# A new hand-written order for the five instruction queues of a clustered attention kernel with a spatial gating layer

## The chip, the cores and the metric

The kernel runs on one core of one Trainium2 chip. The metric is the device time of one execution in microseconds (us). The kernel before took 648.02 us, the median of 3 runs (647.39 to 654.46). TensorE is called PE here, VectorE DVE, ScalarE ACT, GpSimd POOL, and SyncE, which issues nearly all DMAs, SP.

## The reference

Two stages follow each other. First an attention in which a query sees only the keys of its own cluster (4 batches, 8 heads, 768 rows, 64 columns), then a gated layer on the joined heads.

```python
q_assign = argmax(einsum('bhsd,hcd->bhsc', q_n, c_n))   # 16 clusters a head
k_assign = argmax(einsum('bhsd,hcd->bhsc', k_n, c_n))
mask = q_assign[:, :, :, None] == k_assign[:, :, None, :]
scores = where(mask, 0.125 * q @ k.T, -1e9)
attn = softmax(scores)
x = (attn @ v)            # heads joined: 4 x 768 x 512
h = relu(x @ w_in)        # 512 -> 1024
u, v = h[..., :512], h[..., 512:]
v_n = (v - mean(v)) / sqrt(var(v) + 1e-6)
v_s = einsum('ts,bsd->btd', w_spatial, v_n) + b_spatial
out = (u * v_s) @ w_out
```

## The kernel before, in words

The work is cut into 16 head pairs, four a batch, numbered 0 to 15. For each pair `prep` loads q, k and v, splits them into float16 high and low parts, finds the clusters by small matmuls (lines 708 to 710, "logits") and DVE steps (lines 727 to 731), and has ACT write the one-hot codes into `ohx` (lines 739 and 740). For the first heads `shifts` computes a bound on the scores first: matmuls of line 826, one DVE maximum each (line 833), a last reduction (line 845) and its way into `hq` (lines 846, 849, 863, 864). `attend` then makes the attention in tiles of 128 rows by 768 columns, six a head. There are two kinds of tile:

- 108 tiles of the earlier heads: scores (lines 923 and 925), exponential on ACT (929), float16 copy on ACT (931), low part on POOL (932), then 18 matmuls with v (937, "values").
- 84 tiles of the later heads (the list `ROW`), which take their maximum over a row of the scores: scores (lines 887 and 889), DVE maximum (892 to 894), exponential on ACT into a `p32` buffer (895), copy on ACT (897), low part on POOL (898), a transposing DMA issued by SP from `pt` back into the same `p32` buffer (903), then 18 matmuls with v (907). In the trace `p32` is called p. There are four `p32` buffers: the exponential of a tile has to wait until the values of the tile four before it have been read.

`mlp` does the gated layer of a batch once its four pairs have their transposed x. Its matmuls all have line 982 (a helper), in chunks of six matmuls of 128x512: v and u (from xT and win), the spatial product (from vn and wsp, then DVE 1046, ACT 1047, POOL 1048 and a transposing DMA 1049), and the output product (from gT, in the last batch from a `pt` buffer, and wou; then ACT 1059 and the output DMA 1060). The chunks of batch b are spread between the attention tiles of batch b+1; those of the last batch stand alone at the end.

Every piece of work is recorded as an operation with its engine (`op`), and nothing is issued until `plan.run()`. A table `ORDER` then gives, for each of the five queues, the order in which its operations are issued, as numbers: the k-th recorded operation of that engine. PE has 799 operations, ACT 738, DVE 908, POOL 294, SP 355. `run` walks through the queues with its own estimate of start times, which only decides which PSUM buffer (of four `acc` and two `sc`) an operation gets; the order within a queue is the table's.

```python
own = [o for o in self.ops if o.eng == e]
queue[e] = [own[int(k)] for k in ORDER.get(e, "").split()][::-1]
```

An engine runs its queue in order. An operation that waits holds up all that stands behind it on its engine.

Of the kernel before, what the change touches and what calls it, by code (L numbers as in the profile page):

```python
# [151 lines left out]
""",  # L152
    "ACT": """
# [16 lines left out]
""",  # L170
    "DVE": """
# [960 lines left out]
```

## Time and profile before

| what | value |
|---|---|
| time, median of 3 runs | 648.02 us (647.39 to 654.46) |
| time of the profiled execution | 652.16 us |
| its span, first to last instruction | 650.4 us |
| PE busy | 598.9 us, 92% of the span |
| ACT, DVE, POOL busy | 456.1 us, 436.4 us, 429.7 us |
| mean granted clock of PE, as a share of 2.4 GHz | 0.99 |

The profile is one execution on the chip. The table says how long each engine worked, not what set the end: PE is the busiest, and the 51 us in which it did nothing are spread over the span. The rows further down show where.

### The profile page before, as it was taken

Reading aid. Unit: us, or ns where it says so; the run is one execution under the profiler, and the core shown is the slowest. Engines: PE = TensorE matmul, PEld = TensorE weight load, DVE = VectorE, ACT = ScalarE, POOL = GpSimd, SP = SyncE. Lnnn points to the kernel's source line nnn. Section 1 sums busy time; section 2 is a strip of 40 time slices with the busy share of each in tenths; the row PEclk is TensorE's granted clock in tenths of the full one; section 3 lists DMA queues with packets and bytes.
Section 4 is the critical chain, followed back from the end, with each engine's and each line's share of the span. In section 5 each row is a group of like instructions: output and inputs, shape, how many; then the busy total and the mean of one; then the engine's idle time right before and its main releaser. Section 6 shows DMA issues by size and latency. Waiting matters only on the chain.

```text
span 650.4 us, 16379 instructions
## 1 busy us (share of the span) xinstructions
PE 598.9 (92%) x6509; PEld 355.9 (55%) x6509; DVE 436.4 (67%) x935; ACT 456.1 (70%) x713; POOL 429.7 (66%) x305
## 2 busy tenths in 40 slices
PE   3798998799999999988999999889989999899996
PEld 2475766566555655555665566555555555444442
DVE  7899999998879884768785646658556556123110
ACT  5688999798777767768789788776868787233122
POOL 2468999789477956668688879665868677323210
PEclk9999999799989999999999999999999999899999
DMA  6566676656744999899868799999999999900215
GB/s 196 126 171 158 164 160 141 163 129 156 175 84 142 189 209 175 180 170 196 164 147 164 142 228 180 203 188 163 186 200 195 197 187 179 153 33 16 43 41 145
DMA packets 225645, 101.38 MB, mean 156 GB/s; under 512 B 210320, under 2 KB 211936, under 8 KB 225568
## 3 DMA queue, kind: packets, MB, share of 16 engines
q1 hardware_dynamic: 221824, 93.65, 72.9%
q10 hardware_dynamic: 3744, 6.69, 3.1%
q8 instruction: 51, 0.84, 0.5%
q14 instruction: 26, 0.21, 0.1%
HBM read 27.63 MB, written 6.29 MB: 52 GB/s over the span
## 4 chain that ended last, share of the span: by engine, by line
PE 35%; DMA 14%; ACT 4%; issue 3%; DVE 3%; POOL 2%; SPq 1%; POOLq 0%; ACTq 0%; DVEq 0%
PE acc L982 22%; DMA p<-pt 11%; PE acc L907 5%; PE sc L887 2%; PE sc L889 2%; PE acc L937 2%; DMA gT<-ghl 2%; ACT p L895 1%; DMA pt<-ghl 1%; POOL pt L898 1%; DVE rs L892 1%; ACT pt L897 1%; PE sc L923 1%; PE sc L925 1%; PE acc L826 0%
## 5 line engine op out<-in xcount | busy, mean ns | idle before, releaser
L932 POOL TENSOR_TENSOR pt<-p,pt 128x768 f16<-128x768 f32 x108 | 185.5, 1736 | 38.7 <-ACT pt L931 20.3
L898 POOL TENSOR_TENSOR pt<-p,pt 128x768 f16<-128x768 f32 x84 | 139.6, 1665 | 67.7 <-ACT pt L897 41.2
L982 PE MATMUL acc<-win,xT 128*128 128x512 f16 x576 | 134.4, 379 | 0.3 <-DMA xT<-xhl 0.3
L892 DVE TENSOR_REDUCE rs<-sc 128x1 f32<-128x768 f32 x84 | 80.1, 954 | 55.3 <-PE sc L889 53.3
L895 ACT ACTIVATE p<-sc,rs 128x768 f32<-128x768 f32 x84 | 83.0, 990 | 43.7 <-DVE rs L894 22.6
L833 DVE TENSOR_REDUCE nm<-acc 128x1 f32<-128x512 f32 (+1 forms) x162 | 104.8, 680 | 12.1 <-PE acc L826 11.8
L982 PE MATMUL acc<-vn,wsp 128*128 128x512 f16 x432 | 101.1, 379 | 0.0
L929 ACT ACTIVATE p<-sc 128x768 f32<-128x768 f32 x108 | 85.6, 805 | 14.2 <-PE sc L925 7.0
L931 ACT CAST pt<-p 128x768 f16<-128x768 f32 x108 | 87.7, 828 | 2.4 <-PE acc L937 2.0
L982 PEld LDWEIGHTS <-xT 128*128 128x128 f16 x576 | 54.9, 97 | 60.9 <-DMA xT<-xhl 0.8
L937 PEld LDWEIGHTS <-pt 128*128 128x128 f16 x1944 | 71.2, 99 | 10.8 <-issue 1.2
L937 PE MATMUL acc<-vhl,pt 128*128 128x65 f16 (+1 forms) x1944 | 75.4, 195 | 0.0
L907 PEld LDWEIGHTS <-p 128*128 128x128 f16 x1512 | 55.2, 97 | 33.8 <-DMA p<-pt 21.5
L907 PE MATMUL acc<-vhl,p 128*128 128x65 f16 x1512 | 59.4, 193 | 13.4 <-DMA p<-pt 13.3
L897 ACT CAST pt<-p 128x768 f16<-128x768 f32 x84 | 69.7, 830 | 1.7 <-PE acc L937 0.3
L826 PE MATMUL acc<-hq 80*128 80x512 f16 (+1 forms) x216 | 60.4, 351 | 10.8 <-DVE nm L833 4.4
L982 PEld LDWEIGHTS <-wsp 128*128 128x128 f16 x432 | 40.9, 97 | 44.8
L982 PE MATMUL acc<-wou,gT 128*128 128x512 f16 x216 | 53.1, 388 | 3.8 <-DMA gT<-ghl 3.8
L923 PE MATMUL sc<-hq,lo 128*128 128x512 f16 x216 | 55.6, 340 | 0.5 <-ACT p L929 0.4
L925 PE MATMUL sc<-hq 81*128 81x512 f16 x216 | 55.3, 338 | 0.2 <-DVE hq L864 0.2
L1048 POOL TENSOR_TENSOR ghl<-u,ghl 128x512 f16<-128x512 f32 x24 | 28.3, 1186 | 40.7 <-ACT ghl L1047 39.4
L1046 DVE SCALAR_TENSOR_TENSOR u<-acc,bsp,u 128x512 f32<-128x512 f32 x24 | 18.0, 748 | 51.5 <-PE acc L982 51.3
(125 smaller groups left out, 873.8 us busy)
## 6 DMA issues: line engine op xcount, KB each, us to landing
raw<-in_kqT_dram SPq DMA_DIRECT2D x15, 768.0 KB
vraw<-in_vp_dram SPq DMA_DIRECT2D x16, 384.0 KB
hq<-hq SPq DMA_DIRECT2D x15, 384.0 KB
out_dram<-gT ACTq DMA_DIRECT2D x18, 256.0 KB
hq<-lo SPq DMA_DIRECT2D x16, 192.0 KB
lo<-hq SPq DMA_DIRECT2D x16, 192.0 KB
wraw<-in_wsT_dram SPq DMA_DIRECT2D x6, 384.0 KB
vn<-in_w_in_dram SPq DMA_DIRECT2D x4, 512.0 KB
```

Of the source, the lines that this page charges most:

```text
L833: V.tensor_reduce(out=nm.t[:, t, k:k + 1] if n == 1 else nm.t[:, t:t + n, k], in_=src, axis=AX.X, op=ALU.max, negate=True)
L892: o = op("DVE", 0.95, lambda sc=sc, rs=rs: V.tensor_reduce(out=rs.t[:, 0:1], in_=sc.t[:, 0:S], axis=AX.X, op=ALU.max, negate=True), after= ...
L895: o = op("ACT", 0.99, lambda sc=sc, p32=p32, rs=rs: A.activation(out=p32.t, in_=sc.t[:, 0:S], func=AF.Exp, bias=rs.t[:, 2:3], scale=rs.t[: ...
L897: o = op("ACT", 0.83, lambda pt=pt, p32=p32: A.copy(out=pt.t[:, 0, :], in_=p32.t), after=[o], use=[p32], new=[pt], key=K_HI)
L898: o = op("POOL", 1.65, lambda pt=pt, p32=p32: G_.tensor_tensor(out=pt.t[:, 1, :], in0=p32.t, in1=pt.t[:, 0, :], op=ALU.subtract), after=[o ...
L907: T.matmul(out=av.t[:, k * (D + 1):k * (D + 1) + w], lhsT=rt()[:, c, :], rhs=rhs, skip_group_check=True, **f)
L923: T.matmul(out=sc.t[:, cs], lhsT=lo.t[:, h, ks], rhs=hq.t[:, 2, h, cs], start=True, stop=False)
L929: o = op("ACT", 0.81, lambda sc=sc, p32=p32: A.activation(out=p32.t, in_=sc.t[:, 0:S], func=AF.Exp, bias=P_LOG * LN2, scale=SC_UNIT), afte ...
L931: o = op("ACT", 0.83, lambda pt=pt, p32=p32: A.copy(out=pt.t[:, 0, :], in_=p32.t), after=[o], use=[p32], new=[pt], key=K_HI)
L932: o = op("POOL", 1.65, lambda pt=pt, p32=p32: G_.tensor_tensor(out=pt.t[:, 1, :], in0=p32.t, in1=pt.t[:, 0, :], op=ALU.subtract), after=[o ...
L937: T.matmul(out=av.t[:, t * (D + 1):t * (D + 1) + w], lhsT=lhsT, rhs=rhs, skip_group_check=True, **f)
L982: T.matmul(out=acc.t, lhsT=lr[m][0], rhs=lr[m][1], start=(m == 0), stop=(m == n - 1))
```

## The change

All five lists of numbers in `ORDER` are replaced by others. The order was searched for anew over replays in which DMA landings, loads and issue times were scattered. No operation, tile, buffer or constant is changed: each list holds the same numbers as before. The last two lines of POOL's list stand for the rest (the lists are 3094 numbers in all):

```diff
     "POOL": """
...
-270 257 272 273 264 274 275 276 277 219 220 271 221 278 279 281 280 222 282 283 284 285 287 286 288 289 290 292 291 293
+270 272 257 273 264 274 275 276 277 271 219 220 221 278 222 279 280 281 282 283 284 285 287 286 288 289 290 291 292 293
```

What this moves is seen in the queues themselves. Three places follow.

First place: ACT near the start, where pair 1's codes (lines 740 and 739, which read `acc1` and so give it back) meet the load of pair 2 (line 668 reads `raw`, which a DMA fills). The kernel before:

```order
L846 ACTIVATE shx0_84<-nl_361 128x6
L849 ACTIVATE shx0_84<-nl_361 128x6 x2
L668 ACTIVATE hq_380<-raw_310 128x768
L740 ACTIVATE ohx_83<-acc1_111 128x6x2x16
L739 ACTIVATE ohx_83<-acc1_111 128x6x2x16
L929 ACTIVATE p32_390<-sc1_109 128x768
```

The changed kernel at the same place:

```order
L793 ACTIVATE wl0_93<-w32_259 2x2x65
L740 ACTIVATE ohx_83<-acc1_111 128x6x2x16
L739 ACTIVATE ohx_83<-acc1_111 128x6x2x16
L668 ACTIVATE hq_383<-raw_312 128x768
L929 ACTIVATE p32_400<-sc0_108 128x768
```

The two code writes moved from behind line 668 to before it.

Second place: PE in pair 14, the first tile of its first head, just ahead of that tile's values (line 907; p32_8239 and p32_8241 are the tile's buffer in the one kernel and the other). The kernel before:

```order
L889 LDWEIGHTS hq_6512
L889 MATMUL sc1_109<-hq_6512 128x512
L889 LDWEIGHTS hq_6512
L889 MATMUL sc1_109<-hq_6512 128x256
L907 LDWEIGHTS p32_8239
L907 MATMUL acc0_110<-vhl0_87,p32_8239 128x65
```

The changed kernel, directly ahead of the same tile's values:

```order
L982 LDWEIGHTS wsp_105
L982 MATMUL acc1_111<-vn_107,wsp_105 128x512
L982 LDWEIGHTS wsp_105
L982 MATMUL acc1_111<-vn_107,wsp_105 128x512
L907 LDWEIGHTS p32_8241
L907 MATMUL acc2_112<-vhl0_87,p32_8241 128x65
```

A chunk of the gated layer now stands between those scores and the values.

Third place: the end of POOL's queue, the low parts of the last batch's six gated tiles 0 to 5. In the kernel before u32_9576 is tile 3 and u32_9694 tile 4:

```order
L1048 TENSOR_TENSOR ghl_9617<-u32_9542,ghl_9617 128x512
L1048 TENSOR_TENSOR ghl_9635<-u32_9517,ghl_9635 128x512
L1048 TENSOR_TENSOR ghl_9659<-u32_9578,ghl_9659 128x512
L1048 TENSOR_TENSOR ghl_9740<-u32_9694,ghl_9740 128x512
L1048 TENSOR_TENSOR ghl_9719<-u32_9576,ghl_9719 128x512
L1048 TENSOR_TENSOR ghl_9781<-u32_9716,ghl_9781 128x512
```

In the changed kernel u32_9560 is tile 3 and u32_9695 tile 4:

```order
L1048 TENSOR_TENSOR ghl_9630<-u32_9461,ghl_9630 128x512
L1048 TENSOR_TENSOR ghl_9632<-u32_9584,ghl_9632 128x512
L1048 TENSOR_TENSOR ghl_9665<-u32_9582,ghl_9665 128x512
L1048 TENSOR_TENSOR ghl_9730<-u32_9560,ghl_9730 128x512
L1048 TENSOR_TENSOR ghl_9766<-u32_9695,ghl_9766 128x512
L1048 TENSOR_TENSOR ghl_9784<-u32_9732,ghl_9784 128x512
```

Before, tile 4 stood ahead of tile 3; now they stand in their own order. On SP the transposing DMAs of tiles 3, 4 and 5 are the last three in both kernels, in that order.

## Rows read from the trace of the kernel before

**Rows 1.** The page, busy time of the engines over the whole span.

```profile
PE 598.9 (92%) x6509; PEld 355.9 (55%) x6509; DVE 436.4 (67%) x935; ACT 456.1 (70%) x713; POOL 429.7 (66%) x305
```

**Rows 2.** Busy time by stretch: length, busy us (x count), PE clock, DMA share, GB/s.

```profile
0.00:32.00 32.00, 18.42 (x138) 10.24 (x139) 24.99 (x81) 19.44 (x33) 11.42 (x23) 1.00 0.59 162
32.00:150.00 118.00, 106.55 (x1611) 75.05 (x1610) 116.27 (x215) 105.74 (x186) 102.37 (x63) 0.97 0.66 156
400.00:560.00 160.00, 150.63 (x1627) 88.21 (x1622) 95.41 (x234) 117.33 (x156) 112.27 (x79) 1.00 1.07 189
560.00:650.40 90.40, 82.50 (x372) 36.59 (x372) 15.21 (x39) 20.94 (x37) 18.89 (x18) 0.98 0.27 60
```

**Rows 3.** Waits, whole span: who waited for whom, us in total, times, longest.

```profile
ACT p L895 <- PE acc L907: 16.5, 15, 2.4
...
PE acc L907 <- DMA p<-pt: 13.3, 15, 2.0
```

**Rows 4.** The chain that ended last, 400 to 560 us: start, us, what.

```profile
451.05 5.48 DMA p<-pt
456.57 0.71 PE acc L907 x18
457.61 0.33 PE sc L889 x2
457.94 1.30 PE acc L982 x6
```

**Rows 5.** The page, costliest groups: busy us, mean ns of one, idle before.

```profile
L898 POOL TENSOR_TENSOR pt<-p,pt 128x768 f16<-128x768 f32 x84 | 139.6, 1665 | 67.7 <-ACT pt L897 41.2
...
L895 ACT ACTIVATE p<-sc,rs 128x768 f32<-128x768 f32 x84 | 83.0, 990 | 43.7 <-DVE rs L894 22.6
...
L897 ACT CAST pt<-p 128x768 f16<-128x768 f32 x84 | 69.7, 830 | 1.7 <-PE acc L937 0.3
```

**Rows 6.** Timeline, 26 to 29 us: start, us, instruction, idle before and its releaser.

```profile
26.42 0.84 ACT L668 ACTIVATE hq<-raw 128x768 f16<-128x768 f32 x1 [3.00 <-DMA raw<-in_kqT_dram]
...
27.88 1.01 PE L826 MATMUL acc<-hq 80*128 80x512 f16 x3 [1.55 <-ACT ohx L739]
...
28.50 0.69 DVE L833 TENSOR_REDUCE nm<-acc 128x1 f32<-128x512 f32 x1 [1.10 <-PE acc L826]
```

**Rows 7.** Timeline, 556 to 563 us.

```profile
556.00 9.16 SPq L1049 DMA_TRANSPOSE gT<-ghl  x3
...
562.02 9.63 PE L982 MATMUL acc<-wou,gT 128*128 128x512 f16 x36 [2.66 <-DMA gT<-ghl]
```

**Rows 8.** Timeline, the tail, 624 to 646 us.

```profile
624.04 0.61 ACT L1047 CAST ghl<-u 128x512 f16<-128x512 f32 x1
...
628.30 0.62 ACT L1047 CAST ghl<-u 128x512 f16<-128x512 f32 x1 [3.65 <-issue]
...
629.00 2.27 POOL L1048 TENSOR_TENSOR ghl<-u,ghl 128x512 f16<-128x512 f32 x2 [13.12 <-ACT ghl L1047]
...
631.29 9.02 SPq L1049 DMA_TRANSPOSE pt<-ghl  x3
...
637.86 4.06 PE L982 MATMUL acc<-wou,pt 128*128 128x512 f16 x18 [1.46 <-ACT ghl L1047]
...
642.16 4.06 PE L982 MATMUL acc<-wou,pt 128*128 128x512 f16 x18 [0.25 <-DMA pt<-ghl]
```

**Rows 9.** Timeline, 107 to 116 us: one long DVE instruction and POOL beside it.

```profile
107.76 6.44 POOL L932 TENSOR_TENSOR pt<-p,pt 128x768 f16<-128x768 f32 x4
...
110.82 4.20 DVE L765 SCALAR_TENSOR_TENSOR vhl<-vraw,vhl 128x768 f16<-128x768 f32 x1
...
115.67 0.58 PE L826 MATMUL acc<-hq 80*128 80x512 f16 x1 [2.86 <-DVE nm L833]
```

**Rows 10.** All instructions of line 765: min/median/max ns, first and last start.

```profile
L765 DVE SCALAR_TENSOR_TENSOR vhl<-vraw,vhl x14: 905/957/4198, 59.2 to 524.5; 128x768 f16<-128x768 f32 x14
```

**Rows 11.** Busy time in the stretch after that instruction (columns as in Rows 2).

```profile
116.00:124.00 8.00, 7.38 (x72) 4.82 (x71) 6.93 (x8) 6.66 (x12) 5.14 (x3) 0.60 0.65 128
```

128 rows, old and new, of the table ORDER are left out of this document.

## The prediction

> **What bounds the kernel now.** I read four views, in this order. The page's busy times: PE works 598.9 us [rows 1] of a span of 650.4 us, so a new order, which removes no work, can at most win back the 51.5 us that PE stands idle, plus what matmuls lose at the lower clock. The busy time by stretch says where that idle time lies [rows 2]. In the first 32 us PE works only 18.4 us, since everything waits for the first loads and the first clusters. From 32 to 150 us PE idles 11.4 us, and the engine that is full is DVE: 116.3 of 118 us. From 400 to 560 us PE idles 9.4 us and no engine is full. From 560 us on, PE is alone with the last gated layer and idles 7.9 us. Third, the waits: between 217 and 560 us the largest wait of PE itself is for the transposed tiles, 13.3 us in 15 waits, 0.89 us each [rows 3]. Fourth, the chain that ended last and the timeline, to see what stands behind single waits.
>
> So there are two kernels in one. Up to 150 us DVE sets the pace; after that PE does, and each wait of PE adds its length to the end.
>
> **The change part by part.** It adds and removes nothing; each term is a wait that gets shorter or longer. I counted through both orders with the durations of the rows: 0.65 us for a tile's scores (four matmuls, two of them 0.33), 1.30 for a chunk of six, 0.55 for a tile's values (the 0.71 of the row is until the last has drained; their starts lie 0.55 apart) [rows 4].
>
> *Head.* ACT stood 3.00 us in front of line 668, waiting for the load of pair 2, with the two code writes behind it in the queue. These free an `acc` buffer, so PE's line 826 waited 1.55 us for them, and then DVE 1.10 us for PE [rows 6]. In the new order the code writes stand ahead of line 668 (first place shown), and DVE no longer has that hole. DVE is what is full from here to 150 us, so I carry its 1.10 us to the end: -1.1. Bounds: -1.55, PE's whole wait, to +0.84: the new order also puts an ACT copy (line 680) in front of the very first head's code writes and rows, and an ACT instruction of that size takes 0.84 [rows 6].
>
> *The DVE stage, 32 to 150 us.* I counted the DVE work that stands ahead of each pair's last result in both orders: the same for pair 3, whose result closes this stage (145 us of instructions in both). 0. What a different neighbour on POOL can do here is a rival below.
>
> *Waits for transposed tiles.* This is the largest term. Between the scores and the values of the same tile PE has other work, and the tile's way (DVE maximum, exponential 0.99, copy 0.83, low part 1.67, transposing DMA 5.48) must fit into it [rows 4, 5]. Counted over the 84 tiles this work is 13.3 us in the mean before and 14.25 after, and 12.7 against 14.4 in the median: the new order leaves each tile some 1 to 1.7 us more. Second place shown: there 10.0 becomes 13.1. If each of the 15 waits got 0.95 us shorter, nearly all of the 13.3 us would go; that is one end. But the four `p32` buffers limit it: ACT's exponential waited 16.5 us in 15 waits for values that had not yet been read [rows 3], and where that decides, later values only make a later exponential. I went through the 15 tiles: in eight the work grows and the exponential had not waited for a buffer; in the other seven it stays, shrinks (18.8 to 13.5, 13.8 to 11.3) or the buffer decides. Half of 13.3 is 6.7; and the faster PE gets, the closer the next wait is, so I take -4. Bounds -13.3 to +5 (the other seven and as many more growing by 0.7 us, in the middle of the waits seen).
>
> *Before the last layer.* At 562.02 PE had waited 2.66 us for a transposing DMA of the gated layer, the first of three that were in flight together [rows 7]. The spatial product that feeds it ends one place (1.30 us) earlier on PE in the new order. POOL and SP in front of that DMA are full with attention tiles, so little of it gets through: -0.5; bounds -2.66 to 0.
>
> *Tail.* Before, tile 3's copy was there at 624.65, but POOL's queue had tile 4 ahead of it, whose copy began only at 628.30. POOL started both at 629.00, so tile 3's DMA was issued at 631.29 together with tile 4's, tile 5's copy waited for a `ghl` buffer, and PE waited 1.46 and 0.25 us, its last product starting at 642.16 [rows 8]. In the new order POOL takes tile 3 first, and its DMA is long over. But tile 4's spatial product now ends three chunks (3.9 us) later on PE, so its DMA is issued near 634.1 and tile 5's near 636.6, where PE needs them at 637.5 and 640.1. How long such a DMA takes is bounded by the same rows: tile 4's, issued right behind tile 3's, let PE start at 637.86, at most 6.6 us after 631.29; tile 5's, whose issue is over by 640.31 (631.29 and 9.02), let it start at 642.16, at least 1.9 after. With 1.9 PE waits for neither, -1.7; with 6.6 it starts on tile 5 at 643.2 instead of 642.16, +1.0; with the 5.48 of an attention tile's DMA [rows 4] nothing changes. The two are now 2.5 us apart and tile 3's is out of their way, so I take -1.0.
>
> *Sum.* -1.1 - 4 - 0.5 - 1.0 = -6.6 us. Against the profiled execution, 652.16 us, that would be 645.6. That execution is 4.1 us longer than the median of the runs shown, and it has one accident that is about as large: a DVE instruction of line 765 took 4.20 us instead of the median 0.957, in the stage where DVE is full, and PE stood 2.86 us behind it [rows 9, 10]. I take it that the median run lacks this, and put the sum against the median: 648.0 - 6.6 = 641.4 us.
>
> **A rule weighed.** The long instruction of line 765 began at 110.82 and ended at 115.02, while POOL ran four instructions from 107.76 to 114.20, 1.61 each, without a break [rows 9]; it lasted past the ends of at least two of them. The Trainium skill (SBUF — State Buffer, "Who interferes with whom") says that a DVE instruction with both inputs in SBUF contends with a GpSimd instruction that reads SBUF, and that the second to start is blocked until the first is finished. By that rule one such meeting would cost at most one POOL instruction, 1.61 us; the trace shows 3.24 (4.20 less 0.957), so the trace's number is used below.
>
> **The rivals.**
>
> *The waits come back (644).* PE's wait is only the last link: the loop over a `p32` buffer is 0.99 + 0.83 + 1.67 + 5.48 + 0.71 = 9.7 us [rows 4, 5], and between a tile's values and those four tiles later PE has under 10 us of work at 27 of 80 places before and still at 20 after. Then a third of the gain stays, near 1 us in place of 4: 648.0 - 1.1 - 1 - 0.5 - 1.0 = 644.4. For it: the DMA share of 1.07 in 400 to 560 us [rows 2]. Against it: eight of the 15 waits had a free buffer. Chance 0.18.
>
> *Nothing comes of it (648).* The waits are scatter: a DMA that lands late hits another tile, and a new order moves the holes without removing them. For it: the runs of one kernel spread over 7 us, as much as the sum. Against it: the tail and the head are waits of order, not of scatter. Chance 0.12.
>
> *DVE locked out more often (slower, 654).* In 32 to 150 us DVE has 1.7 us to spare [rows 2], and POOL is busy 102 of 118 us. Two more meetings like that of line 765, which stands two places later in DVE's queue in the new order beside the same run of POOL, cost 2 x 3.24 = 6.5 us, and PE then falls to the lower of its two levels, 1.2 GHz, as it did from 116 to 124 us (granted 0.60) after standing idle for 2.86 us [rows 9, 11]: 648 + 6.5 = 654.5 with nothing gained elsewhere. It decides from the second such meeting on. Against it: 13 of the 14 instructions of line 765 were near 0.96 us [rows 10]. By the skill's rule it would be 648 + 2 x 1.61 = 651.2. Chance 0.12.
>
> **How the numbers follow.** About 1% (6.5 us) is what a measurement of this kernel can tell from no change; the line between faster and the same is 641.5. My forecast of 641.4 has a chance of 0.55, with a range of its own of 634 to 646; it lies at the line, but where the largest term is off it has more room above (13.3 against the 4 taken), so I give 0.40 of it to faster and 0.15 to the same. The returned waits give 0.15 to the same and 0.03 to faster; nothing gives 0.10 to the same and 0.02 to slower; the lock-outs 0.12 to slower. A gain of most of the 13.3 us (near 632) has the last 0.03. Faster 0.46, same 0.40, slower 0.14. The range, 632 to 652, leaves out some of the lock-outs and of the large gains.
>
> **What would show it.** In the changed kernel's profile: line 826 no longer waits for line 739 near 27 us; PE's line 907 waits for DMA p<-pt well under 13.3 us in all, 6 to 10, with the same DMA durations; the last low parts on POOL are apart, and and the wait before the last products is shorter than 1.46 us. I am wrong if the waits of line 907 are as large as before, if PE's idle time between 32 and 150 us grows by more than 3 us, or if the sum of PE's idle time falls while its busy time rises by as much, which would be the lower clock.

## The result and the profile after

The changed kernel takes 624.26 us (median of 4 runs, 622.17 to 626.47) where the kernel before took 649.2 beside it: a ratio of 0.960, 95% interval 0.953 to 0.967. Ratios leave out executions more than 1.5% longer than the fastest of the same kernel, so they are not always the quotient of the medians beside them. Forecast were 641.4 us and a range of 632 to 652: the direction was right, the time lies below the range, and the gain is 25 us instead of 6.6.

The profiled execution of the changed kernel took 625.61 us, its span is 623.5, 26.9 less than before. First the page's busy line and the busy time by stretch (columns as in [rows 2]):

```profile
PE 592.1 (95%) x6509; PEld 354.4 (57%) x6509; DVE 432.6 (69%) x935; ACT 456.6 (73%) x713; POOL 421.7 (68%) x305
```

```profile
0.00:32.00 32.00, 18.91 (x144) 10.77 (x145) 26.86 (x86) 19.29 (x33) 10.65 (x22) 1.00 0.66 181
32.00:150.00 118.00, 109.88 (x1676) 77.21 (x1674) 115.39 (x216) 110.63 (x192) 103.06 (x67) 0.99 0.67 163
150.00:222.00 72.00, 71.96 (x756) 42.14 (x753) 63.91 (x125) 55.30 (x94) 51.80 (x36) 1.00 0.62 155
222.00:400.00 178.00, 176.86 (x2110) 108.84 (x2109) 124.22 (x263) 145.74 (x221) 135.81 (x95) 1.00 0.95 186
400.00:560.00 160.00, 155.13 (x1564) 88.88 (x1563) 92.01 (x224) 111.17 (x151) 107.60 (x77) 1.00 0.97 174
560.00:623.50 63.50, 59.40 (x275) 26.56 (x273) 10.21 (x24) 14.45 (x26) 12.82 (x12) 0.99 0.26 67
```

The two stretches of the kernel before that [rows 2] leave out:

```profile
150.00:222.00 72.00, 70.33 (x786) 42.85 (x784) 60.31 (x115) 55.21 (x93) 53.07 (x36) 0.98 0.63 144
222.00:400.00 178.00, 170.45 (x1990) 102.97 (x1989) 124.21 (x256) 137.43 (x212) 131.73 (x90) 1.00 0.90 178
```

Length less PE's busy time is its idle time. It fell from 13.6 to 13.1 us ahead of 32 us, from 11.4 to 8.1 up to 150, from 18.6 to 6.0 between 150 and 560, and from 7.9 to 4.1 behind: 20.2 us in all. The other 6.7 are busy time, 598.87 against 592.14 with the same 6509 matmuls. Two PE groups that show it (busy us, mean ns of one, idle before), before:

```profile
L925 PE MATMUL sc<-hq 81*128 81x512 f16 x216 | 55.3, 338 | 0.2 <-DVE hq L864 0.2
L982 PE MATMUL acc<-wou,gT 128*128 128x512 f16 x216 | 53.1, 388 | 3.8 <-DMA gT<-ghl 3.8
```

and after:

```profile
L925 PE MATMUL sc<-hq 81*128 81x512 f16 x216 | 53.9, 331 | 0.0
...
L982 PE MATMUL acc<-wou,gT 128*128 128x512 f16 x216 | 51.5, 379 | 1.9 <-DMA gT<-ghl 1.9
```

The same instructions are shorter in the mean. PE was more often granted the higher of its two levels (in the stretch 32 to 150 us 0.99 instead of 0.97). Worked out from the mean granted clock, 0.990 over 650.4 us and 0.996 over 623.5, the two profiles lost 6.5 and 2.5 us to it; by this estimate it makes some 4 of the 6.7, and the rest is not explained. The profile of the kernel before is also one of its longer executions. e6 (below), whose time is that of the kernel before, has 595.6 us busy and 50.3 idle in a span of 645.9: beside it the difference in idle time is 18.9 us and that in busy time only 3.5.

The waits that answer to [rows 3], whole span:

```profile
ACT p L895 <- PE acc L907: 17.9, 18, 2.1
...
PE acc L907 <- DMA p<-pt: 3.0, 4, 1.1
```

PE's wait for the transposed tiles has almost gone (13.3 to 3.0), while ACT waits for a free `p32` buffer as long as before (16.5 to 17.9).

The two profiled executions lie 3.0 and 1.4 us over their kernels' medians (652.16 over 649.2, 625.61 over 624.26), so 1.6 us of what lies between them is their own. Over all comparisons the kernel before ran between 640.6 and 657.3 us, the changed kernel between 622.2 and 626.5.

The 25 us are at the high end. In the five later comparisons the kernel before has medians of 645.5 to 648.8, and e8, as fast as the changed kernel, has a ratio of 0.970 (0.966 to 0.973), some 20 us. The time of the kernel before goes with the granted clock of the execution: of its 83 runs there, the four with a mean of 0.998 or more took 640.6 to 642.5 us, the nine with 0.987 or less 652.1 to 657.3. The 18 with 0.996 or more have a median of 644.1 us, and the changed kernel's four runs, all at 0.996 or more, one of 624.3. These runs were not side by side, but at about the same clock the gain is then 20 us, by as much as PE's idle time fell.

### The profile page after: what moved, and what is told of

Same layout as the page of the kernel before. It is cut to its first block, busy times and chain, and to the rows that moved or that the text cites. A ratio compares the mean times of both kernels' runs of the same rounds, so it can differ in the third digit from the quotient of the medians.

```text
span 623.5 us, 16411 instructions
## 1 busy us (share of the span) xinstructions
PE 592.1 (95%) x6509; PEld 354.4 (57%) x6509; DVE 432.6 (69%) x935; ACT 456.6 (73%) x713; POOL 421.7 (68%) x305
## 4 chain that ended last, share of the span: by engine, by line
PE 47%; DMA 6%; issue 3%; ACT 2%; POOL 2%; DVE 0%; POOLq 0%; ACTq 0%; DVEq 0%
PE acc L982 28%; PE acc L907 6%; DMA p<-pt 4%; PE sc L887 3%; PE sc L889 3%; PE acc L937 3%; PE sc L923 1%; DMA pt<-ghl 1%; PE sc L925 1%; DMA gT<-ghl 1%; PE acc L826 1%; ACT p L895 1%; POOL pt L898 1%; ACT pt L897 1%; POOL ghl L1048 1%
## 5 line engine op out<-in xcount | busy, mean ns | idle before, releaser
L932 POOL TENSOR_TENSOR pt<-p,pt 128x768 f16<-128x768 f32 x108 | 178.9, 1678 | 34.4 <-ACT pt L931 15.6
L898 POOL TENSOR_TENSOR pt<-p,pt 128x768 f16<-128x768 f32 x84 | 138.3, 1651 | 54.2 <-ACT pt L897 31.6
L895 ACT ACTIVATE p<-sc,rs 128x768 f32<-128x768 f32 x84 | 83.1, 990 | 40.3 <-PE acc L907 17.9
L937 PEld LDWEIGHTS <-pt 128*128 128x128 f16 x1944 | 71.0, 98 | 13.4 <-issue 1.9
L982 PEld LDWEIGHTS <-wsp 128*128 128x128 f16 x432 | 40.7, 97 | 44.9 <-issue 0.2
L923 PE MATMUL sc<-hq,lo 128*128 128x512 f16 x216 | 53.8, 330 | 1.8 <-ACT p L929 1.5
L925 PE MATMUL sc<-hq 81*128 81x512 f16 x216 | 53.9, 331 | 0.0
L982 PE MATMUL acc<-wou,gT 128*128 128x512 f16 x216 | 51.5, 379 | 1.9 <-DMA gT<-ghl 1.9
```

Of the source, the lines that this page charges most:

```text
L895: o = op("ACT", 0.99, lambda sc=sc, p32=p32, rs=rs: A.activation(out=p32.t, in_=sc.t[:, 0:S], func=AF.Exp, bias=rs.t[:, 2:3], scale=rs.t[: ...
L898: o = op("POOL", 1.65, lambda pt=pt, p32=p32: G_.tensor_tensor(out=pt.t[:, 1, :], in0=p32.t, in1=pt.t[:, 0, :], op=ALU.subtract), after=[o ...
L932: o = op("POOL", 1.65, lambda pt=pt, p32=p32: G_.tensor_tensor(out=pt.t[:, 1, :], in0=p32.t, in1=pt.t[:, 0, :], op=ALU.subtract), after=[o ...
L937: T.matmul(out=av.t[:, t * (D + 1):t * (D + 1) + w], lhsT=lhsT, rhs=rhs, skip_group_check=True, **f)
L982: T.matmul(out=acc.t, lhsT=lr[m][0], rhs=lr[m][1], start=(m == 0), stop=(m == n - 1))
```

## The experiments

Time is given beside the kernel before of the same comparison. In the diffs a piece of a list in `ORDER` stands for the whole list.

### Where the gain lies: the new order in one stretch only

**e1_early.** All five lists are the changed kernel's up to about 142 us (PE's first 253 numbers; 214 of its places, 173 of ACT's, 212 of DVE's, 99 of SP's and 23 of POOL's are other than before), then the old order.

```diff
 "PE": """
-8 9 10 11 6 16 12 14
+8 11 9 12 13 14 15 6
...
```

> The changed order up to the end of the stage in which DVE is full (about 142 us), from there on the order before. Theory A (most of the gain lies behind 150 us, where the transposed tiles are): a gain of 1 to 8 us, 641 to 648 against 649.2, since by 142 us the two profiles had come apart by only 5 to 7 us, and 3.2 of that is the single DVE instruction of line 765 that took 4.20 us. Theory B (the first stage delays everything and the rest follows): 630 or less. If the 4.20 us of line 765 belongs to the old order rather than to one execution, the gain is 6 to 8 us, if not, 1 to 4.

**e2_late.** The reverse: the old order up to about 145 us (PE's first 238 numbers), then the changed one.

```diff
 "PE": """
...
-297 288 305 308 290 299 310 301
+297 275 288 305 290 299 308 311
...
```

> The order before up to about 145 us, from there on the changed order. Theory A: 628 to 634, a gain of 15 to 21 us, with PE's waits of line 907 for the transposed tiles at 2 to 5 us as in the changed kernel. Theory B: 640 or more.

**e10_mid.** The same with the seam at 340 us (PE's first 494 numbers are old).

```diff
 "PE": """
...
-420 521 427 530 421
+420 530 538 421 521 427
...
```

> The order before up to 340 us, the changed order from there. Theory A, evenly spread (each stretch in which all five queues are new gives its share): the profiles of before and after are 15 us apart by there and 26 at the end, so this kernel is 9 to 13 us faster than before, 636 to 640. If the gain comes from one place ahead of 340 us, such as the crowd of DMA issues at 262 to 285 us: within 4 us of before.

Measured: e1 644.2 against 646.9, ratio 0.998 (0.993 to 1.002); e2 634.3 against 646.9, 0.982 (0.972 to 0.992); e10 637.8 against 647.4, 0.987 (0.980 to 0.995). The busy time by stretch shows where. The kernel before, from 150 to 340 and from 340 to 560 us:

```profile
150.00:340.00 190.00, 181.48 (x2054) 109.39 (x2052) 149.05 (x295) 141.59 (x230) 134.88 (x91) 0.99 0.80 165
340.00:560.00 220.00, 209.93 (x2343) 124.63 (x2341) 130.88 (x309) 168.39 (x230) 162.19 (x113) 1.00 1.03 187
```

e1_early, old order in both stretches:

```profile
150.00:340.00 190.00, 184.62 (x2072) 111.11 (x2071) 152.63 (x309) 144.16 (x233) 135.78 (x92) 1.00 0.79 164
340.00:560.00 220.00, 209.03 (x2298) 122.93 (x2297) 124.50 (x292) 163.26 (x224) 158.39 (x111) 0.99 1.01 182
```

e2_late, new order in both:

```profile
150.00:340.00 190.00, 187.22 (x2129) 112.94 (x2128) 151.67 (x309) 149.42 (x242) 138.51 (x95) 1.00 0.80 173
340.00:560.00 220.00, 215.81 (x2349) 128.00 (x2346) 130.40 (x304) 166.05 (x227) 161.72 (x114) 0.99 1.03 186
```

e10_mid, old order in the first, new order in the second:

```profile
150.00:340.00 190.00, 180.17 (x2049) 108.93 (x2046) 148.85 (x296) 143.06 (x233) 136.34 (x92) 1.00 0.80 169
340.00:560.00 220.00, 215.83 (x2376) 128.10 (x2375) 133.06 (x309) 169.59 (x231) 163.03 (x114) 1.00 1.03 187
```

PE idles 8.5 and 10.1 us before, 5.4 and 11.0 in e1, 2.8 and 4.2 in e2, 9.8 and 4.2 in e10. Where all five lists are new, PE idles 1.0 to 5.0 us a stretch (1.0 and 5.0 in the changed kernel), where they are old 5.4 to 11.0, whatever stood ahead of the seam. That is theory A, evenly spread; theory B falls. e1's 5.4 is the lowest of the old ones and 3 us under the kernel before, with the same lists there: that much is scatter, or left over from the stretch before. By their ratios e1 and e2 gain 1.4 and 11.8 us (e2 5 to 18, where 15 to 21 were expected), some 13 together and less than the whole. In PE's idle time over the whole span they do add: 51.5 us before, 44.9 in e1, 38.1 in e2 and 31.4 in the changed kernel, so 6.6 and 13.4 of the 20.2. The seams, where lists meet that weren't made for each other, therefore cost no idle time that these profiles show. The spread of the runs (639.7 to 649.0 for e1) is the nearest reason for the rest; it was not tried apart.

### Which list carries it

**e3_after_old_sp** and **e4_before_new_sp**: only SP's list is exchanged, in the changed kernel and in the one before. e4 (e3 is its mirror):

```diff
 "SP": """
-0 1 20 21 2 27
+0 20 21 1 2 27
...
```

> The changed kernel with the DMA issues of SP put back into the old sequence (one pair of its 849 exchanged pairs stays exchanged); the other four queues are those of the changed kernel. Theory S (the gain comes from SP: a transposing DMA no longer stands behind one that is not ready): 636 or more, most of the gain lost, and the waits of line 907 back above 9 us. Theory P (the gain comes from PE: each tile has more work between its scores and its values): 629 or less, waits of line 907 under 6 us.

> The kernel before with the DMA issues of SP in the new sequence (three pairs stay exchanged); the other four queues are the old ones. Theory S: 637 or less, waits of line 907 under 6 us. Theory P: 645 or more, waits of line 907 still 9 us or more.

**e11_pe_sp_new** and **e12_act_dve_pool_new**: the halves {PE, SP} and {ACT, DVE, POOL}, each as far as the other half's old lists allow. e11 changes 606 of PE's 799 places and e4's list of SP, e12 615 of ACT's, 718 of DVE's and 134 of POOL's:

```diff
 "ACT": """
-20 22 21 32 33 23
+20 21 32 4 33 24
...
```

> The kernel before with PE's and SP's lists drawn towards the changed order as far as the old lists of the other three allow (of 1221 exchanged pairs on PE 422 stay old, of 849 on SP 3); ACT, DVE and POOL are exactly the old ones. Theory PS (room on PE and issue on SP together make the gain): 636 or less. Theory F (all five lists fit one another, and a part of them gives nothing): 648 or more, above 660 if old ACT and DVE lists make the moved issues wait as in the kernel with only SP's list new (708.5).

> The other half: ACT, DVE and POOL drawn towards the changed order (of 1496, 1620 and 113 exchanged pairs 151, 402 and 3 stay old), PE and SP exactly the old ones. Theory PS: 645 or more, waits of line 907 above 9 us. Theory F: slower than before as well, 655 or more. If the order of ACT, DVE and POOL makes the gain: 636 or less.

Measured: e3 680.4 us, ratio 1.058 (1.050 to 1.065); e4 708.5, 1.099 (1.090 to 1.107); e11 820.3, 1.270 (1.262 to 1.277); e12 775.5, 1.200 (1.192 to 1.209). Theory S foretold e3 and failed at e4, where the new issues of SP alone cost 60 us; theory P failed at e3; theory PS failed at e11. What a list does when its neighbours are of the other order shows in the waits of e11, whole span:

```profile
POOL pt L898 <- ACT pt L897: 84.4, 32, 13.1
DVE rs L892 <- PE sc L889: 78.2, 44, 11.5
...
DVE nm L833 <- PE acc L826: 67.2, 42, 8.2
...
PE sc L887 <- ACT p L895: 34.9, 22, 3.4
```

All four have grown (before they are 41.2, 53.3, 11.8 and 0.4 us). That each engine stands in front of work that comes later in another one's list is my reading of it, not shown by itself. Neither SP's list nor either half carries the gain; theory F, that the lists have to fit, is what these runs leave. But the halves are mixtures (in e11 a third of PE's exchanged pairs stay old): they show what new lists cost beside foreign ones, not what a list is worth among its own, and the list of PE, ACT, DVE or POOL was not exchanged by itself. Nor do they say in what the fit consists. The next runs tried that.

### What removes the waits for the transposed tiles

**e5_values_later**, **e6_issue_when_ready**, **e7_both**: repairs of the kernel before at the places where it waited. In e5 the number moved back is a tile's values, in e6 the one moved ahead a transposing DMA.

```diff
 "PE": """
...
-364 366 247 368
+364 247 366 368
...
 "SP": """
...
-202 19 147 148
+202 147 19 148
...
```

> The kernel before with only PE's list changed, and only at the 15 places where line 907 waited for its transposed tile: there the tile's values stand one to three places later, behind as much PE work (0.65 to 3.24 us) as the wait had lasted. Theory P (what PE has to do between scores and values decides): the 13.3 us of these waits fall under 4, and the time by 8 to 12 us, to 637 or less. Theory R (the loop over the p32 buffers decides, and the waits come back one tile later): waits of line 907 still 9 us or more, time within 4 us of before.

> The kernel before with only SP's list changed: 24 transposing DMAs of line 903 that the trace shows issued 0.6 us or more after their tile was ready are put ahead of the 30 other DMA issues (13 of them line 755) that SP took up in between. Theory S: the mean from the end of POOL's low part to the issue falls from 1.01 us to about 0.6, the waits of line 907 from 13.3 to under 7, the time by 5 to 9 us. Theory P: the waits stay above 9 us and the time within 3 us of before.

> The kernel before with the edits of both kernels above. If each tile's way and its room add, the waits of line 907 fall under 2.5 us, and the time to 632 to 636, which is where the order before up to 145 us with the changed order behind it stood (634.3). If one of the two does it all, the time is that of the better one of them.

Measured: e5 652.0 against 648.8, 1.012 (1.008 to 1.016); e6 648.9, 1.000 (0.995 to 1.005); e7 649.3, 1.011 (1.001 to 1.020). The waits of e5 (us in total, times, longest):

```profile
ACT p L895 <- PE acc L907: 24.5, 20, 2.6
...
PE acc L907 <- DMA p<-pt: 13.8, 15, 2.4
```

13.8 us in 15 waits, as before; but none of them is one of the old 15. At all 15 edited tiles PE no longer waits, and it waits at other tiles instead, eight of them the very next one (tile by tile, from PE's starts). ACT waits 24.5 us for buffers instead of 16.5. That is the prediction's rival "the waits come back". It is the edit that moved them, not chance: in e9, e15 and e16 (below), which have the old lists there, 12 of the old 15 tiles wait again, 13.0, 11.3 and 12.5 us in all. In e6 the mean from the end of POOL's low part to the issue fell from 1.01 to 0.56 us (over the 84 tiles; 0.59 in the changed kernel) and the waits of line 907 to 9.3 (8.6 in e7), but nothing of it reached the end. So half of theory S's chain holds (earlier issue, fewer waits, though not under the 7 us expected), the last link doesn't.

**e8_after_issue_when_ready**: the same on SP in the changed kernel.

```diff
 "SP": """
...
-155 19 145 147 148
+155 147 19 145 148
...
```

> The changed kernel with the same kind of edit on SP by its own trace: 11 transposing DMAs that were issued 0.6 us or more after their tile was ready go ahead of 16 other DMA issues. PE's waits of line 907 are only 3.0 us there, so by every theory the gain is small: 0 to 3 us, 621 to 624; slower only if one of the moved loads becomes late.

625.0 us (623.5 to 626.9), the same as the changed kernel's 624.3 in its own comparison. None of the kernels tried here was faster than the changed one.

**e13_all_values_later** and **e14_all_later_and_issue** give every tile the room that it has in the new order.

```diff
 "PE": """
...
-242 362 364 366 247 368 384
+242 247 362 364 366 384 368
...
```

> The kernel before with only PE's list changed: the values of all 84 transposed tiles stand one place later (behind a chunk of the gated layer 35 times, behind scores 47 times, behind other work twice), so that PE has 15.08 us of work between a tile's scores and its values in the mean instead of 13.95; the changed kernel has 14.90. Theory room: the waits of line 907 fall from 13.3 to under 6 us and the time by 6 to 10 us, to 638 to 642. Theory loop (a p32 buffer is given back later by as much): ACT's waits for PE at line 895 grow from 16.5 to above 25 us, the waits on PE come back at lines 887 and 907, and the time is within 4 us of before or longer.

> The same, and the 24 transposing DMAs issued when ready as well. Theory room: under 640. Theory loop: the earlier issue shortens nothing but the waits on PE; the time within 4 us of before, ACT's waits at line 895 above 22 us.

Measured: e13 651.9 against 648.0, 1.007 (1.003 to 1.012); e14 656.9, 1.013 (1.005 to 1.020). The waits of e13:

```profile
ACT p L895 <- PE acc L907: 32.4, 32, 3.3
...
PE sc L887 <- ACT p L895: 11.7, 16, 1.4
...
PE acc L907 <- DMA p<-pt: 2.9, 4, 1.2
```

The wait for the transposed tiles is 2.9 us in 4 waits, just as in the changed kernel, and the time is longer than before. Values that come later give their `p32` buffer back later, so ACT's exponential waits 32.4 us instead of 16.5, and PE waits 11.7 us at the next scores, whose `sc` buffer that exponential has to read. Theory loop holds, for an edit on PE alone.

**e17_later_with_reserve** gives the room only where the loop has some left, **e18_before_rebuilt** joins all edits that had helped.

```diff
 "PE": """
...
-362 364 366 247 368 384
+362 247 364 366 384 368
...
```

> As e13, but values are moved one place later at only 67 of the 84 tiles: where at least 1.8 us of PE work stay between them and the scores that wait for the exponential four tiles on. Room in the mean 14.82 us (13.95 before, 14.90 in the changed kernel). Theory reserve: waits of line 907 under 6 us, PE's waits at line 887 under 4, ACT's at line 895 under 24, time 638 to 643. If it is the other lists after all that must change with it: waits come back as in e5 and e13, within 4 us of before or longer.

> e17 with the 24 transposing DMAs issued when ready, and with the two edits of e9 (code writes ahead on ACT, tile 3 first on POOL). If the terms add: 4.8 from e9 and 5 to 10 from e17: 632 to 638. If e17 gives nothing: 643 to 650, the gain of e9 alone.

Measured: e17 647.3 against 645.5, 1.002 (0.997 to 1.006); e18 645.0, 1.000 (0.997 to 1.003). The waits of e17:

```profile
ACT p L895 <- PE acc L907: 21.1, 21, 3.5
...
PE acc L907 <- DMA p<-pt: 6.4, 10, 1.6
...
PE sc L887 <- ACT p L895: 2.7, 7, 0.7
```

The waits came out nearly as theory reserve said (6.4 where under 6 was expected, 2.7, 21.1), the time did not: it is that of the kernel before. So the reserve is not the missing reason either, or not it alone; and the parts that e18 joins don't add, not even the gain of e9's edits, which are in it. PE's idle time from 150 to 560 us shows it: 18.6 us before, 16.1 in e17, 21.1 in e18 and 6.0 in the changed kernel. In e18 line 907 waits 4.8 us, but line 887 now waits 5.2, and the rest lies at lines 826, 923 and 982.

### Head and tail

**e9_head_tail**, **e15_head**, **e16_tail**: the two edits that the prediction priced by themselves, together and apart.

```diff
 "ACT": """
...
-37 82 46 45 56
+37 46 45 82 56
...
 "POOL": """
...
-290 292 291 293
+290 291 292 293
```

> The kernel before with only two edits: on ACT the two code writes of pair 1 (lines 740 and 739) ahead of line 668, and on POOL tile 3's low part ahead of tile 4's at the very end. By the prediction's terms the head gives 1.1 us and the tail 1.0: 645 to 647 against 648.8, too little for the median to show; so it is read in the profile. Head: in the first 32 us DVE's wait for PE's line 826 falls from 2.1 us to under 1, and DVE is busy 26 us there instead of 24.9. Tail: PE's waits for the last copies fall from 1.7 us (1.46 and 0.25) to under 1.

> Only the two code writes of pair 1 ahead of line 668 on ACT. Prediction's term: 1.1 us. If the 4.8 us of both edits together lie mostly here (DVE's work up to 150 us comes at another time against POOL's, and the long instruction of line 765 stays away): 3 us or more. In the profile DVE waits 1.0 us for line 826 in the first 32 us instead of 2.1.

> Only tile 3's low part ahead of tile 4's at the end of POOL's list. Prediction's term: 1.0 us (bounds -1.7 to +1.0); the waits of the last layer for copies (1.46 and 0.25 us) gone. If the 4.8 us lie mostly here: 3 us or more, which those two waits do not hold.

Measured: e9 642.6 against 647.4, 0.993 (0.989 to 0.998), a gain of 4.8 us; e15 647.2 against 648.0, 0.999 (0.995 to 1.003); e16 644.9 against 648.0, 0.995 (0.991 to 0.999), 3.1 us. DVE's wait for line 826 in the first 32 us is 2.1 us before; in e15:

```profile
DVE nm L833 <- PE acc L826: 1.0, 1, 1.0
```

At DVE the head does what was said of it, 1.1 us. Of PE's waits behind 555 us the kernel before has these, and e16 only the first, with 1.9:

```profile
PE acc L982 <- DMA gT<-ghl: 2.7, 1, 2.7
PE acc L982 <- ACT ghl L1047: 1.5, 1, 1.5
PE acc L982 <- DMA pt<-ghl: 0.2, 1, 0.2
```

POOL taking tile 3 first removes the 1.7 us of the other two, the far end of the tail's bounds; the interval of e16 (0.4 to 5.9 us) holds that. The sum of e15 and e16 is 3.9, e9 gives 4.8: they agree within their intervals.

## Why the prediction was wrong

**What was right.** PE's idle time is what there was to win, no work went away, and the waits for the transposed tiles were its largest part. Of the signs asked for, the wait ahead of the last products is short, and the waits of line 907 fell even below the 6 to 10 us that I gave; none of the signs against me appeared. One sign that I asked for failed, at the head.

**Head, -1.1.** The wait of DVE fell as said (e15), but line 826 still waits. In the changed kernel, 25 to 28 us:

```profile
25.78 1.01 PE L826 MATMUL acc<-hq 80*128 80x512 f16 x3 [1.12 <-ACT ohx L739]
...
26.69 2.48 DVE L833 TENSOR_REDUCE nm<-acc 128x1 f32<-128x512 f32 x4
27.59 0.84 ACT L668 ACTIVATE hq<-raw 128x768 f16<-128x768 f32 x1 [1.86 <-DMA raw<-in_kqT_dram]
```

Line 826 still waits 1.12 us for line 739; what went is DVE's hole behind it [rows 6], and ACT's wait for the load stands where nobody is behind it. As a gain the term looks too small: in the first 150 us PE is busy 128.1, 127.5 and 128.3 us in the three kernels that have this edit and otherwise the old order up to there (e9, e15, e18), and 125.5 in the mean of the ten without it that follow below: 2.5 us more. The time of e15 can't confirm that (a gain of 0.8 us, interval -1.8 to 3.2).

**The DVE stage, 0.** I took the same sum of DVE work ahead of pair 3's result as the same time. In the two profiles PE worked 3.3 us more between 32 and 150 us. Part of it is the long instruction of line 765, which I called an accident that the median run lacks. All instructions of line 765 (min/median/max ns, first and last start) in e2_late, another execution with the old order in this stage:

```profile
L765 DVE SCALAR_TENSOR_TENSOR vhl<-vraw,vhl x14: 905/958/4191, 62.8 to 496.7; 128x768 f16<-128x768 f32 x14
```

and in the changed kernel:

```profile
L765 DVE SCALAR_TENSOR_TENSOR vhl<-vraw,vhl x14: 919/983/2542, 56.5 to 486.8; 128x768 f16<-128x768 f32 x14
```

4.19 us, as 4.20 in [rows 10], and both times it is the third of the 14; among ten executions whose first 145 us are in the old order it appeared in these two. So the median run does lack it, as I took it, but it isn't scatter alone. (That 13 of the 14 were near 0.96 us I read into the median: four others took 1.34 to 1.67.) Over these ten PE's busy time in the first 150 us is 123.0 to 126.6 us, mean 125.5; in the changed kernel and e8 it is 128.8 and 128.3. Of this difference of 3 us the head's edit alone makes 2.5, so the 0 for the rest of the stage was off by about half a microsecond.

**Waits for transposed tiles, -4.** The largest term was mis-sized: the waits fell by 10.3 us, PE's idle time between 150 and 560 us by 12.5. The step that failed is the halving: I judged tile by tile that in seven of 15 the wait would stay because the room or the buffer decides, and took 4 as what is left. In the changed kernel only one of the 15 still waits (1.07 us), beside three tiles that had not; the two that I named as shrinking (18.8 to 13.5, 13.8 to 11.3) do not wait. The waits belong to the order as a whole: they return at the same tiles while the lists stay (e9, e15, e16), and e5 shows that they move to the neighbour when their own tiles are mended, so counting the 15 places could neither prove a gain nor deny one. My reason for the gain, more room on PE, failed as well: e13 gives the same room and gains nothing. And I put a change of the tile's own way at nothing: from the end of its scores to the end of SP's issue it took 10.65 us before and 10.09 after (mean of the 84 tiles, from the traces), 0.42 us of the difference in front of SP's issue. That is not the reason by itself either: e6 has 10.16 and gains nothing. The far bound, -13.3, would have been the better value, but not for the reason I had.

**The rival "the waits come back".** Its mechanism is real (e5, e13: ACT's waits at line 895 grow to 24.5 and 32.4 us) and it decides when PE's list changes by itself. In the changed kernel it did not decide, since ACT's waits stayed at 17.9. Theory F says why only in general: the other four lists moved along. Which of their moves keeps the loop short is open.

**Before the last layer, -0.5; tail, -1.0.** The wait of 2.66 us at 562 us [rows 7] is absent from the changed kernel, and from e2 and e10, which have the new order there. With the old order there it stays, at the same chunk of line 982: 1.65 us in e9, 1.95 in e15, 1.94 in e16, 1.17 in e1. In e9 it stands at 552.96 us; among PE's waits from 150 to 560 us, beside those for the transposed tiles:

```profile
PE acc L907 <- DMA p<-pt: 13.0, 15, 2.5
...
PE acc L982 <- DVE xn L958: 1.6, 1, 1.6
```

(The releaser is the one that came last by the profile; the chunk reads `gT`.) So this wait is the order's, 1.2 to 2.7 us, and -0.5 took too little of it; the bound of -2.66 held. The tail's 1.7 us became 0.4:

```profile
615.75 4.06 PE L982 MATMUL acc<-wou,pt 128*128 128x512 f16 x18 [0.41 <-DMA pt<-ghl]
```

The two terms together, -1.5, stand against 3.8 us less idle time behind 560 us.

**What the sum left out.** 6.7 of the 26.9 us between the two profiles are busy time (3.5 beside e6's profile), and no term stood for it. Each wait counted only its own length, although [rows 11] had shown what follows one: the lower level for a time. At the second such place, behind the 2.66 us, the kernel before shows

```profile
562.00:570.00 8.00, 7.98 (x30) 3.30 (x31) 0.00 (x0) 1.63 (x3) 2.02 (x2) 0.79 0.48 92
570.00:578.00 8.00, 8.00 (x39) 3.64 (x38) 1.38 (x3) 2.28 (x4) 0.00 (x0) 1.00 0.00 0
```

30 matmuls where the next 8 us hold 39, at a granted clock of 0.79 against 1.00.

**Nothing of it, and DVE locked out.** Both fell: scatter did not restore the waits, which come back at the same tiles only with the old lists, and line 765 took 2.54 us at worst instead of 4.20. The Trainium skill (SBUF — State Buffer, "Who interferes with whom") says that the second of the two to start is blocked while the first runs. Read as in the prediction, that would cost a DVE instruction at most one of POOL's, 1.61 us here; it lost 3.24 and 3.23 in the two executions, so the measurement stands.

**What stays open.** That PE's idle time falls stretch by stretch with all five lists, and that SP's list alone or a mixture for either half of the five brings no gain, is shown (e1 to e4, e10 to e12). Which property of the whole makes it is not: room on PE, early issue on SP and a reserve in the `p32` loop each removed waits as foreseen, and none of them, nor all together (e18), shortened the kernel by a measurable amount. One rival was not tried: which PSUM buffer an operation gets is settled while the lists are walked, so it changed with them, and no run held it fixed.

## What to carry to other kernels

Where several in-order queues share small rings of buffers, expect a wait that you remove at one place to turn up elsewhere: here it came at other tiles (e5), at the ring's other end (e13) or at other lines (e18). Price a new order by the idle time of a stretch, not by adding up waits, and keep the full idle time of the stretch as a likely end of the range. Exchanging one list, or a part of the five, between the two orders cost 6 to 27% here; whole stretches of all queues could be taken over. Compare times at the same granted clock where you can, and add to a wait what the engine loses behind it at the lower level.

## What the runs showed of the hardware

The long DVE instruction repeats to within a hundredth of a microsecond: 4.198 and 4.191 us in two executions of different kernels at the same place of the order, the third of the 14; in the other eight executions it took 0.99 to 1.01 us seven times and 1.90 once. The changed order has such places too: the third took 2.54 us in the changed kernel, the fourth 2.85 in e1 and 2.84 in e8. My reading is a meeting with POOL's work that the order makes possible and small shifts in time bring about or avoid. And SP's part of a transposing DMA is not short: over the 84 of line 903 in the kernel before

```profile
L903 SPq DMA_TRANSPOSE p<-pt x84: 1274/1677/3623, 226.7 to 554.2; - x84
```

it held SP's queue for 1.27 to 3.62 us each, and in that time no other DMA of SP was issued.
